# Exponentials ahead of the copies of transposed probabilities, and the softmax's multiply ahead of their low parts, in a kernel of window attention and two feed-forward blocks

## The chip, the core and the metric

The kernel runs on one core of a Trainium2 chip. The metric is the device time of one execution in microseconds; the kernel before takes 861.66 us, the median of three runs (861.57 to 862.0).

## What is computed

Attention with a window of 64 positions over 4 sequences of 576 tokens and 8 heads of 64, then two feed-forward parts on the 2304 tokens. All is in 32-bit floats.

```python
scores = scale * np.matmul(q, k.transpose(0, 1, 3, 2))
mask = (rel >= 0) & (rel < window)
scores = np.where(mask, scores, -1000000000.0)
scores = scores - np.max(scores, axis=-1, keepdims=True)
attn = np.exp(scores)
attn = attn / (np.sum(attn, axis=-1, keepdims=True) + 1e-09)
x = np.matmul(attn, v)
...
a = x @ w1
b = x @ w2
h = a * b @ w3
x = h @ w_out
...
h = x @ w_in
g = h * (1.0 / (1.0 + np.exp(-h)))
out = g @ w_out2
```

## The kernel before

**Precision.** Most matrix products are made in three passes of a faster 32-bit format: an operand is split into a high part (a rounded copy, made on ScalarE) and a low part (operand minus high part, made on VectorE or GpSimd), and high x high, high x low and low x high are added up in PSUM. In the trace the high parts are CAST instructions, the low parts TENSOR_TENSOR instructions with a subtraction.

**Attention** goes in 72 groups: a group is 128 queries of one pair of heads against 192 keys, and 12 groups are one block of 384 tokens. Groups 0 to 16 are plain: their products are ordinary 32-bit ones with no low parts. The work of group g is cut into two halves, written by half(h):

- The even half of g issues scores(g) on TensorE (L272, L276, or L268 in plain groups) and their masked maxima on VectorE (L282); values(g - 2), the product of transposed probabilities pt and values (L349, L350, or L342 to L344); the three transposes of g - 1 into the PSUM tile t (L315); split_t(g - 1), which copies t to pt on ScalarE (L325, L327) and takes the low parts on VectorE (L328, two of L330), or in plain groups one copy to pw (L321); and exps(g), the two exponentials on ScalarE (L293).
- The odd half of g issues normalise(g) on VectorE: a reduction (L301), a reciprocal (L303) and the multiply of the probabilities by it (L305); then the pending total of values(g - 2): two copies on ScalarE (L357, L358), two sums on VectorE (L359, L360) and one add on GpSimd into xr (L361). Then prep_qk (a cast on ScalarE, L247; low parts on GpSimd, L251, and VectorE, L254), prep_v (vhl: L79 on ScalarE, L82 on GpSimd) and the loads on SyncE's queue. In the last group of a block the total stands in the even half instead, behind the exponentials, because the next block needs xr.

**The rest.** phase_w, the front stage, rebuilds the weights from 64-bit words on ScalarE, VectorE and GpSimd and multiplies w3 with w_out (L492), with 28 halves in between. Then come six blocks of the first feed-forward part, phase_a: 16 units of 12 matmuls (L520) whose product is a = (x w1)(x w2), made on VectorE (L528) and split into p or q by ScalarE (L79) and GpSimd (L82); then 8 units of 12 matmuls (L540) with the combined weights, while the next block's xr is split into xa and xb. Ahead of each unit, unit(n) issues one half of attention, so a block carries 24 halves, 12 groups. The attention ends within the fifth block (block 4); the second feed-forward part (L640, L659) follows and fills the rest.

**Order.** The program is scheduled by hand: every engine runs its instructions in the order in which they are written, and waits at the first whose inputs or buffers are not ready. pt and the probabilities sm have two buffers each, t has one.

Of the kernel before, what the change touches and what calls it, by code (L numbers as in the profile page):

```python
# [14 lines left out]
ALU = mybir.AluOpType  # L15
# [27 lines left out]
def tile_window_attention_ffn(ctx, tc, qkv, vp, mask, ident, w1, w2, w3t, w_out, w_in, w_out2, out):  # L43
# [7 lines left out]
    nc = tc.nc  # L51
# [7 lines left out]
    def f32(ap):  # L59
        return ap.bitcast(F32)  # L60
# [99 lines left out]
    def fill(n=1):  # L160

        for _ in range(min(n, len(parts))):
            parts.pop(0)()
# [24 lines left out]
    NG = NU * NPAIR  # L188
# [14 lines left out]
    HEADS = (0, slice(0, 64)), (1, slice(64, 128))  # L203
# [4 lines left out]
    def plain(g):  # L208


        return g < PLAIN
# [20 lines left out]
    def load_v(g):  # L232
        if g < NG and ("v", g) not in loaded:
            loaded.add(("v", g))
            if plain(g):
                nc.sync.dma_start(out=v_p[g % 3], in_=vp[g])
                return
            v_raw[g] = att.tile([128, 3, 64], F32, name=f"v{g}", tag="v", bufs=3)
            u, c = place(g)
            nc.sync.dma_start(out=v_raw[g].rearrange("p t d -> p (t d)"), in_=qkv[u, c, :, 768:960])  # L240

    def prep_qk(g):
        if g >= NG or plain(g):
            return
        t = qk_raw.pop(g)
        hi = att.tile([128, 768], F32R, name=f"qkhi{g}", tag="qkhi", bufs=2)
        nc.scalar.copy(out=hi, in_=t)  # L247
        q, k = slice(128, 384), slice(384, 768)
        for h, hs in HEADS:
            n = slice(384 + h * 192, 576 + h * 192)  # L250
            nc.gpsimd.tensor_tensor(  # L251
                out=k_lo[g % 2][hs, h * 192 : h * 192 + 192], in0=t[hs, n], in1=f32(hi[hs, n]), op=ALU.subtract
            )
        nc.vector.tensor_tensor(out=hi[64:128, q], in0=t[64:128, q], in1=f32(hi[64:128, q]), op=ALU.subtract)  # L254
        qk_st[g] = hi

    def prep_v(g):
        if plain(g):
            return
        vhl = att.tile([128, 3, 2, 64], F32R, name=f"vhl{g}", tag="vhl", bufs=2)  # L260
        split(vhl[:, :, 0], vhl[:, :, 1], v_raw.pop(g), "act", "pool")
        v_st[g] = vhl

    def scores(g):
        s_ps = psa.tile([128, 2, 192], F32, name=f"s{g}", tag="s")
        t = qk_raw.pop(g) if plain(g) else qk_st.pop(g)
        if plain(g):
            nc.tensor.matmul(s_ps, lhsT=t[:, 0:128], rhs=k_p[g % 2], start=True, stop=True)  # L268
        else:
            for h in range(2):  # L270

                nc.tensor.matmul(  # L272
                    s_ps[:, h], lhsT=t[:, 128 + h * 128 : 256 + h * 128],
                    rhs=t[:, 384 + h * 192 : 576 + h * 192], start=(h == 0), stop=False,
                )
            nc.tensor.matmul(s_ps, lhsT=t[:, 0:128], rhs=k_lo[g % 2], start=False, stop=True)  # L276
        nm = att.tile([128, 2], F32, name=f"nm{g}", tag="nm", bufs=2)
        rs = att.tile([128, 2], F32, name=f"rs{g}", tag="rs", bufs=2)
        fill(2)
        for h in range(2):  # L280

            nc.vector.tensor_tensor_reduce(  # L282
                out=sm[g % 2][:, h, :], in0=s_ps[:, h, :], in1=mask_sb[:, mask_kind(place(g)[0]), 64 - 64 * h : 256 - 64 * h],
                op0=ALU.add, op1=ALU.min, scale=-(D ** -0.5), scalar=3.0e38, accum_out=nm[:, h : h + 1],
            )
        fill()
        s_st[g] = (nm, rs)

    def exps(g):
        nm, rs = s_st[g]  # L290
        for h in range(2):
            x = sm[g % 2][:, h, :]
            nc.scalar.activation(  # L293
                out=x, in_=x, func=AF.Exp, scale=-1.0, bias=nm[:, h : h + 1], accum_out=sums_of[g % 2][:, h, 0:1]
            )

    def normalise(g):
        _, rs = s_st.pop(g)
        x = sm[g % 2]
        fill()  # L300
        nc.vector.tensor_reduce(out=rs, in_=sums_of[g % 2], axis=mybir.AxisListType.X, op=ALU.add)  # L301
        fill()
        nc.vector.reciprocal(out=rs, in_=rs)  # L303
        fill()
        nc.vector.tensor_tensor(out=x, in0=x, in1=rs.unsqueeze(2).to_broadcast([128, 2, 192]), op=ALU.mult)  # L305

    def transposes(g):

        x = sm[g % 2]
        t_ps = psa.tile([128, 384], F32, name=f"t{g}", tag="t")
        x = x.rearrange("p h n -> p (h n)")
        for i, at in enumerate((0, 256, 128)):
            nc.tensor.transpose(t_ps[:, i * 128 : i * 128 + 128], x[:, at : at + 128], id_sb)  # L315
        return t_ps

    def split_t(g, t_ps):
        if plain(g):
            p_st[g] = p_w[g % 2]  # L320
            nc.scalar.copy(out=p_st[g], in_=t_ps[:, 0:320])  # L321
            return
        b, a = pt[g % 2, 1], pt[g % 2, 0]
        own, before = t_ps[:, 0:256].rearrange("p (h n) -> p h n", h=2), t_ps[:, 256:320]
        nc.scalar.copy(out=b[:, :, 0, :], in_=own)  # L325
        for h, hs in HEADS:
            nc.scalar.copy(out=a[hs, h, 0], in_=before[hs])  # L327
        nc.vector.tensor_tensor(out=b[:, :, 1, :], in0=own, in1=f32(b[:, :, 0, :]), op=ALU.subtract)  # L328
        for h, hs in HEADS:
            nc.vector.tensor_tensor(out=a[hs, h, 1], in0=before[hs], in1=f32(a[hs, h, 0]), op=ALU.subtract)  # L330

    def values(g):
        u, c = place(g)
        r = u % 3 * 128

        tag = "z" if done["step"] == len(line) and g % 2 else "o"
        o_ps = psa.tile([128, 2, 2, 128], F32, name=f"o{g}", tag=tag)
        if plain(g):


            v, p, o = v_p[g % 3], p_st.pop(g), o_ps[:, 0, 0]
            nc.tensor.matmul(o, lhsT=v[:, 0:128], rhs=p[:, 0:128], start=True, stop=False)  # L342
            nc.tensor.matmul(o, lhsT=v[:, 64:192], rhs=p[:, 128:256], start=False, stop=False)
            nc.tensor.matmul(o[:, 0:64], lhsT=v[:, 192:320], rhs=p[:, 256:320], start=False, stop=True)  # L344
            return lambda: nc.scalar.copy(out=xr[:, c, r : r + 128], in_=o)
        vhl = v_st.pop(g)
        b, a = pt[g % 2, 1], pt[g % 2, 0]
        for h in range(2):
            nc.tensor.matmul(o_ps[:, h], lhsT=vhl[:, h], rhs=b[:, h], start=(h == 0), stop=False)  # L349
        nc.tensor.matmul(o_ps[:, :, :, 0:64], lhsT=vhl[:, 2], rhs=a, start=False, stop=True)  # L350
        o_ps = o_ps.rearrange("p h t n -> p h (t n)")

        def total():
            t = att.tile([128, 256], F32, name=f"ot{g}", tag="ot", bufs=1)
            if g == NG - 1:
                att.tile([128, 24], F32, name="odd_end", tag="odd_end", bufs=1)
            nc.scalar.copy(out=t[0:64], in_=o_ps[64:128, 0, :])  # L357
            nc.scalar.copy(out=t[64:128], in_=o_ps[0:64, 1, :])  # L358
            nc.vector.tensor_tensor(out=t[0:64], in0=o_ps[0:64, 0, :], in1=t[0:64], op=ALU.add)  # L359
            nc.vector.tensor_tensor(out=t[64:128], in0=o_ps[64:128, 1, :], in1=t[64:128], op=ALU.add)  # L360
            nc.gpsimd.tensor_tensor(out=xr[:, c, r : r + 128], in0=t[:, 0:128], in1=t[:, 128:256], op=ALU.add)  # L361

        return total

    def half(h):

        g, odd = divmod(h, 2)
        if not odd:  # L370
            if g < NG:
                scores(g)
            if 2 <= g <= NG + 1:
                sums.append(values(g - 2))
                if plain(g - 2):
                    sums.pop()()
            if 1 <= g <= NG:
                split_t(g - 1, transposes(g - 1))
            if g < NG:
                exps(g)  # L380
            if sums and (g - 2) % (3 * NPAIR) == 3 * NPAIR - 1:
                sums.pop()()
        else:
            if g < NG:
                normalise(g)
            if sums:
                sums.pop()()
            prep_qk(g + 2)
            if g < NG:
                prep_v(g)  # L390

            for x in range(g + 2, g + 5):
                if plain(x) and x > g + 2:
                    break
                load_qk(x)
            for x in range(g + 1, g + 4):
                if g < (x - 1 if plain(x - 3) else x - 3):
                    break
                load_v(x)

    halves, sums = [0], []

    def halves_to(n):
        while halves[0] < min(n, LAST_HALF):
# [364 lines left out]
```

## Time and profile before

| | |
|---|---|
| median of three runs | 861.66 us |
| the profiled execution, its own time | 861.8 us |
| its span | 860.0 us |
| TensorE matmul, busy | 842.0 us, 98% |
| TensorE weight load, busy | 736.7 us, 86% |
| VectorE, busy | 435.8 us, 51% |
| ScalarE, busy | 497.7 us, 58% |
| GpSimd, busy | 445.0 us, 52% |
| granted TensorE clock | 1.0 of full speed throughout |

Busy time is the share of the span in which an engine worked on instructions; register and waiting instructions don't count. The ends of matmuls are modelled, so that a TensorE that reads as busy may still wait for a fraction of a microsecond; the starts of its weight loads show that better. In the rows, PE is TensorE's matmul, PEld its weight load, DVE is VectorE, ACT ScalarE, POOL GpSimd.

### The profile page before, as it was taken

The numbers are of one execution on the slowest core, as the hardware profiler recorded it, in microseconds if no ns is written. First come the engines' busy times: TensorE is split into PE (matmuls) and PEld (weight loads), VectorE is DVE, ScalarE is ACT, GpSimd is POOL, SyncE is SP. The second block draws the span as 40 slices with busy tenths as digits, with TensorE's granted clock in tenths as the row PEclk, the third lists the DMA queues.
The fourth block names the chain that finished last, engine by engine and source line by source line (L and its number), as shares of the span: only waits on it lengthen the run. The fifth ranks groups of instructions, "written<-read, shape, count | busy, mean of one in ns | idle before, by whom it ended". The sixth has DMA issues, their size and how long they took to land.

```text
span 860.0 us, 13396 instructions
## 1 busy us (share of the span) xinstructions
PE 842.0 (98%) x4362; PEld 736.7 (86%) x4362; DVE 435.8 (51%) x1160; ACT 497.7 (58%) x1243; POOL 445.0 (52%) x494
## 2 busy tenths in 40 slices
PE   5899999999999999999999999999999999999998
PEld 2455799999999999999999888888888888888896
DVE  5979877677777777676465985111111111111111
ACT  5889778788788788787666874222222222222222
POOL 4668666566666666665595886223322232223222
PEclk9999999999999999999999999999999999999999
DMA  8988333333333334330687200200020002000100
GB/s 289 349 272 276 104 105 102 121 93 108 114 93 111 111 94 125 111 94 30 233 326 263 116 1 0 98 1 1 0 98 1 1 0 74 1 1 0 50 1 26
DMA packets 43205, 85.84 MB, mean 100 GB/s; under 512 B 4864, under 2 KB 22528, under 8 KB 43136
## 3 DMA queue, kind: packets, MB, share of 16 engines
q1 hardware_dynamic: 37088, 75.55, 26.7%
q10 hardware_dynamic: 6048, 9.44, 3.0%
q8 instruction: 35, 0.57, 0.3%
q14 instruction: 34, 0.28, 0.1%
HBM read 75.53 MB, written 9.44 MB: 99 GB/s over the span
## 4 chain that ended last, share of the span: by engine, by line
PE 86%; DVE 1%; ACT 1%; issue 1%; POOLq 0%; POOL 0%; ACTq 0%; DVEq 0%
PE h L640 23%; PE o L659 23%; PE ab L520 22%; PE x L540 12%; PE t L315 2%; PE o L349 1%; PE s L272 1%; PE s L276 1%; PE o L350 1%; ACT sm L293 0%; DVE a L528 0%; DVE sm L305 0%; DVE cv_b L128 0%; POOLq L765 0%; DVE hl L144 0%
## 5 line engine op out<-in xcount | busy, mean ns | idle before, releaser
L82 POOL TENSOR_TENSOR g<-sg,g 128x512 fp32r<-128x512 f32 (+1 forms) x80 | 94.7, 1184 | 244.8 <-ACT g L79 217.7
L640 PE MATMUL h<-x2t,hl 128*128 128x512 f32 (+1 forms) x960 | 210.1, 368 | 0.0
L659 PE MATMUL o<-hl,g 128*128 128x512 f32 x864 | 209.7, 390 | 0.1
L640 PEld LDWEIGHTS h<-x2t,hl 128*128 128x128 f32 x960 | 169.3, 188 | 31.2
L646 DVE TENSOR_TENSOR sg<-h,sg 128x512 f32<-128x512 f32 (+1 forms) x80 | 51.1, 638 | 283.7 <-ACT sg L645 283.6
L659 PEld LDWEIGHTS o<-hl,g 128*128 128x128 f32 x864 | 161.1, 188 | 33.5 <-POOL g L82 0.5
L645 ACT ACTIVATE sg<-h 128x512 f32<-128x512 f32 (+1 forms) x80 | 44.4, 555 | 190.0 <-PE h L640 189.7
L520 PE MATMUL ab<-xa,hl 128*128 128x384 f32 x576 | 119.0, 341 | 0.0
L520 PE MATMUL ab<-xb,hl 128*128 128x384 f32 x576 | 115.3, 334 | 0.0
L520 PEld LDWEIGHTS ab<-xb,hl 128*128 128x128 f32 x576 | 101.2, 188 | 0.0
L520 PEld LDWEIGHTS ab<-xa,hl 128*128 128x128 f32 x576 | 99.2, 188 | 0.0
L132 POOL TENSOR_TENSOR cv_b<-cv_b,cv_r 128x512 int32<-128x512 int32 x48 | 73.5, 1531 | 19.1 <-DVE cv_b L128 8.1
L79 ACT CAST g<-sg 128x512 fp32r<-128x512 f32 (+1 forms) x80 | 46.3, 579 | 63.5 <-DVE sg L646 63.5
L361 POOL TENSOR_TENSOR xr<-ot 128x128 f32<-128x128 f32 x55 | 31.6, 575 | 98.3 <-DVE ot L360 67.2
L251 POOL TENSOR_TENSOR klo<-qk,qkhi 64x192 fp32r<-64x192 f32 x110 | 67.4, 613 | 7.6 <-ACT qkhi L247 2.7
L540 PE MATMUL x<-p,wp 128*128 128x384 f32 x360 | 68.0, 339 | 0.0
L293 ACT ACTIVATE sm<-sm,nm 128x192 f32<-128x192 f32 x144 | 64.5, 450 | 3.9 <-DVE nm L282 2.5
L540 PEld LDWEIGHTS x<-p,wp 128*128 128x128 f32 x360 | 61.7, 188 | 0.1
L125 DVE TENSOR_SCALAR cv_z<-cv_b 128x512 int32<-128x512 int32 x72 | 49.4, 686 | 15.7 <-ACT cv_b L114 14.7
L114 ACT ACTIVATE cv_b<-words 128x512 f32<-128x512 f32 x72 | 48.3, 671 | 12.2 <-DMA words<-in_w_out 4.6
L128 DVE SCALAR_TENSOR_TENSOR cv_b<-words,cv_z 128x512 int32<-128x512 int32 x72 | 49.5, 687 | 3.3
L115 ACT ACTIVATE cv_r<-words 128x512 int32<-128x512 uint32 x72 | 47.8, 664 | 0.0
(81 smaller groups left out, 1236.5 us busy)
## 6 DMA issues: line engine op xcount, KB each, us to landing
qk<-in_qkv SPq DMA_DIRECT2D x55, 384.0 KB, 3.1
words<-in_w_out SPq DMA_DIRECT2D x24, 512.0 KB, 8.0
words<-in_w3t SPq DMA_DIRECT2D x16, 512.0 KB, 6.4
words<-in_w SPq DMA_DIRECT2D x16, 512.0 KB, 6.4
words<-in_w_in SPq DMA_DIRECT2D x16, 512.0 KB, 6.7
v<-in_qkv SPq DMA_DIRECT2D x55, 96.0 KB, 2.7
x2d<-x2s ACTq DMA_DIRECT2D x24, 192.0 KB, 1.9
out_x<-osb ACTq DMA_DIRECT2D x18, 256.0 KB, 2.1
```

The costliest lines, as they stand in the source:

```text
L82: (nc.vector if eng_lo == "dve" else nc.gpsimd).tensor_tensor(out=lo, in0=src, in1=f32(hi), op=ALU.subtract)
L114: nc.scalar.activation(out=f32(self.b), in_=f32(self.high), func=AF.Copy, scale=2.0**-112)
L125: nc.vector.tensor_scalar(out=self.z, in0=b, scalar1=3, scalar2=None, op0=ALU.logical_shift_left)
L128: nc.vector.scalar_tensor_tensor(out=b, in0=self.high, scalar=-0x80000000, in1=self.z, op0=ALU.bitwise_and, op1=ALU.bitwise_or)
L132: nc.gpsimd.tensor_tensor(out=x, in0=b, in1=self.r, op=ALU.add)
L251: nc.gpsimd.tensor_tensor(out=k_lo[g % 2][hs, h * 192 : h * 192 + 192], in0=t[hs, n], in1=f32(hi[hs, n]), op=ALU.subtract)
L293: nc.scalar.activation(out=x, in_=x, func=AF.Exp, scale=-1.0, bias=nm[:, h : h + 1], accum_out=sums_of[g % 2][:, h, 0:1])
L520: nc.tensor.matmul(acc, lhsT=w[:, l, fs], rhs=x[k // 2][:, k % 2, r, :], start=(k == 0 and n == 0), stop=(k == 3 and n == 2),)
L540: nc.tensor.matmul(acc, lhsT=wp[f][:, l, o * 128 : (o + 1) * 128], rhs=p[f][:, r, :], start=(f == 0 and n == 0), stop=(f == 7 and n == 2),)
L640: nc.tensor.matmul(acc, lhsT=weights["in", f // 4, k][:, l, fs], rhs=x[:, k, r, :], start=(k == 0 and i == 0), stop=(k == 3 and i == 2),)
L646: nc.vector.tensor_tensor(out=sg, in0=acc, in1=sg, op=ALU.mult)
L659: nc.tensor.matmul(oacc[t], lhsT=g[:, l, t * 128 : (t + 1) * 128], rhs=weights["out", f][:, r, :], start=(f == 0 and i == 0), stop=(f == 1 ...
```

## The change

half() now calls exps(g) ahead of split_t(g - 1), so that on ScalarE the exponentials stand in front of the copies out of t. split_t issues the copies only and returns its three low parts as a function, low(), which is kept in the list lows; the odd half calls it behind normalise(g). So on VectorE the reduction, reciprocal and multiply of g stand in front of the low parts of g - 1. Plain groups have no low parts, and only ScalarE's order changes in them.

```diff
@@ split_t @@
             p_st[g] = p_w[g % 2]
             nc.scalar.copy(out=p_st[g], in_=t_ps[:, 0:320])
-            return
+            return lambda: None
...
-        nc.vector.tensor_tensor(out=b[:, :, 1, :], in0=own, in1=f32(b[:, :, 0, :]), op=ALU.subtract)
-        for h, hs in HEADS:
-            nc.vector.tensor_tensor(out=a[hs, h, 1], in0=before[hs], in1=f32(a[hs, h, 0]), op=ALU.subtract)
+
+        def low():
+            nc.vector.tensor_tensor(out=b[:, :, 1, :], in0=own, in1=f32(b[:, :, 0, :]), op=ALU.subtract)
+            for h, hs in HEADS:
+                nc.vector.tensor_tensor(out=a[hs, h, 1], in0=before[hs], in1=f32(a[hs, h, 0]), op=ALU.subtract)
+
+        return low
@@ half @@
-            if 1 <= g <= NG:
-                split_t(g - 1, transposes(g - 1))
+            t_ps = transposes(g - 1) if 1 <= g <= NG else None
             if g < NG:
                 exps(g)
+            if t_ps is not None:
+                lows.append(split_t(g - 1, t_ps))
             if sums and (g - 2) % (3 * NPAIR) == 3 * NPAIR - 1:
                 sums.pop()()
         else:
             if g < NG:
                 normalise(g)
+            if lows:
+                lows.pop()()
             if sums:
                 sums.pop()()
```

The line numbers in the orders of the changed kernel are its own: its L330 and L332 are the low parts (L328 and L330 before), L361 to L364 the total (L357 to L360 before), L533 and L535 are L526 and L528 before.

VectorE in one group of block 2, from the low parts of one group (those of t_2200) to the maxima of the next. First before, then now; a name's number only tells buffers apart.

```order
L328 TENSOR_TENSOR pt_976<-t_2200,pt_976 128x2x128
L330 TENSOR_TENSOR pt_974<-t_2200,pt_974 64x64 x2
L301 TENSOR_REDUCE rs_2193<-es_81 128x2
L303 RECIPROCAL rs_2193<-rs_2193 128x2
L305 TENSOR_TENSOR sm_72<-sm_72,rs_2193 128x384
L359 TENSOR_TENSOR ot_2230<-o_2196,ot_2230 64x256
L360 TENSOR_TENSOR ot_2230<-o_2196,ot_2230 64x256
L254 TENSOR_TENSOR qkhi_2236<-qk_2092,qkhi_2236 64x256
```

```order
L301 TENSOR_REDUCE rs_2193<-es_81 128x2
L303 RECIPROCAL rs_2193<-rs_2193 128x2
L305 TENSOR_TENSOR sm_72<-sm_72,rs_2193 128x384
L330 TENSOR_TENSOR pt_976<-t_2200,pt_976 128x2x128
L332 TENSOR_TENSOR pt_974<-t_2200,pt_974 64x64 x2
L363 TENSOR_TENSOR ot_2230<-o_2196,ot_2230 64x256
L364 TENSOR_TENSOR ot_2230<-o_2196,ot_2230 64x256
L254 TENSOR_TENSOR qkhi_2236<-qk_2092,qkhi_2236 64x256
```

The three low parts moved from ahead of the softmax's three steps to behind them, directly ahead of the two sums.

ScalarE in the same group, from the high part of p to the first copy of the total: before, then now.

```order
L79 CAST p_1882<-a_3_2149 128x384
L325 CAST pt_976<-t_2200 128x2x128
L327 CAST pt_974<-t_2200 64x64 x2
L293 ACTIVATE sm_72,es_81<-sm_72,nm_2192 128x192 x2
L526 COPY a_4_2225<-ab_8_2212 128x384
L357 COPY ot_2230<-o_2196 64x256
```

```order
L79 CAST p_1882<-a_3_2146 128x384
L293 ACTIVATE sm_72,es_81<-sm_72,nm_2192 128x192 x2
L325 CAST pt_976<-t_2200 128x2x128
L327 CAST pt_974<-t_2200 64x64 x2
L533 COPY a_4_2222<-ab_8_2209 128x384
L361 COPY ot_2230<-o_2196 64x256
```

The two exponentials moved ahead of the three copies; what stands behind the five is the same. TensorE's, GpSimd's and SyncE's orders are as before.

## Rows read from the trace of the kernel before

**Rows 1.** Busy time by stretch: the stretch, its length, PE, PEld, DVE, ACT, POOL.

```profile
200.00:300.00 100.00, 100.00 (x627) 99.39 (x626) 73.19 (x258) 81.89 (x248) 63.26 (x96) 1.00 0.36 110
```

**Rows 2.** Timeline of one group in block 2: start us, us, engine, line, operation.

```profile
239.67 0.43 DVE L360 TENSOR_TENSOR ot<-o,ot 64x256 f32<-64x256 f32 x1
...
240.18 0.60 POOL L361 TENSOR_TENSOR xr<-ot 128x128 f32<-128x128 f32 x1 [1.85 <-DVE ot L360]
...
241.49 0.37 ACT L325 CAST pt<-t 128x256 fp32r<-128x256 f32 x1
...
242.08 0.60 POOL L82 TENSOR_TENSOR vhl<-v,vhl 128x192 fp32r<-128x192 f32 x1
242.22 0.46 ACT L293 ACTIVATE sm<-sm,nm 128x192 f32<-128x192 f32 x1
242.23 0.42 DVE L328 TENSOR_TENSOR pt<-t,pt 128x256 fp32r<-128x256 f32 x1 [0.64 <-ACT pt L327]
...
242.57 0.45 DVE L330 TENSOR_TENSOR pt<-t,pt 64x64 fp32r<-64x64 f32 x2
...
242.64 1.01 POOL L82 TENSOR_TENSOR p<-a,p 128x384 fp32r<-128x384 f32 x1
...
243.63 0.56 DVE L305 TENSOR_TENSOR sm<-sm,rs 128x384 f32<-128x384 f32 x1
...
244.54 0.37 PEld L349 LDWEIGHTS o<-pt,vhl 128*128 128x128 f32 x2
244.58 0.42 DVE L359 TENSOR_TENSOR ot<-o,ot 64x256 f32<-64x256 f32 x1 [0.39 <-ACT ot L358]
...
244.84 0.19 PEld L350 LDWEIGHTS o<-pt,vhl 128*128 128x128 f32 x1
...
245.01 0.43 DVE L360 TENSOR_TENSOR ot<-o,ot 64x256 f32<-64x256 f32 x1
```

**Rows 3.** Timeline, second half of block 1: a multiply that meets a GpSimd operation.

```profile
215.79 1.02 POOL L82 TENSOR_TENSOR xa<-xr,xa 128x384 fp32r<-128x384 f32 x1
...
216.27 0.95 DVE L305 TENSOR_TENSOR sm<-sm,rs 128x384 f32<-128x384 f32 x1
217.25 0.42 DVE L359 TENSOR_TENSOR ot<-o,ot 64x256 f32<-64x256 f32 x1
```

**Rows 4.** Timeline: the values' last weight load, two groups earlier than in rows 2.

```profile
234.33 0.19 PEld L350 LDWEIGHTS o<-pt,vhl 128*128 128x128 f32 x1
```

**Rows 5.** Timeline, end of the first half of block 2.

```profile
269.32 1.01 POOL L82 TENSOR_TENSOR q<-a,q 128x384 fp32r<-128x384 f32 x1
...
270.38 0.30 PEld L540 LDWEIGHTS x<-q,wp 128*128 128x128 f32 x2 [0.30 <-POOL q L82]
...
271.37 0.19 PEld L350 LDWEIGHTS o<-pt,vhl 128*128 128x128 f32 x1
```

**Rows 6.** Timeline, the seam between blocks 1 and 2.

```profile
223.06 0.56 DVE L305 TENSOR_TENSOR sm<-sm,rs 128x384 f32<-128x384 f32 x1
...
223.82 0.19 PEld L350 LDWEIGHTS o<-pt,vhl 128*128 128x128 f32 x1
```

**Rows 7.** Timeline, end of the front stage: copy and exponentials of a plain group.

```profile
110.31 0.43 ACT L321 COPY pw<-t 128x320 f32<-128x320 f32 x1
...
110.63 0.47 ACT L293 ACTIVATE sm<-sm,nm 128x192 f32<-128x192 f32 x1
```

**Rows 8.** Waits: who waited for whom: us in total, times, longest.

```profile
ACT sm L293 <- DVE nm L282: 2.5, 3, 1.5
...
PE t L315 <- ACT cv_r L115: 1.8, 2, 1.0
PE t L315 <- ACT cv_b L114: 1.6, 1, 1.6
PE t L315 <- DVE sm L305: 1.0, 2, 0.7
```

More of the change, by code (lines that the diff above doesn't have):

```diff
@@ L399, in half @@
                 load_v(x)
-    halves, sums = [0], []
+    halves, sums, lows = [0], [], []
     def halves_to(n):
```

## Prediction, written before the changed kernel was run

> **What bounds the kernel now.** I read the busy share by stretch first. Between 200 and 300 us TensorE is busy all the time and its weight loads fill 99.39 of 100 us, while VectorE shows 73.19, ScalarE 81.89 and GpSimd 63.26 [rows 1]. At first sight nothing that happens on the other three can matter from the first feed-forward block on, and only the front stage, where the weights are rebuilt, has waits on TensorE. The timeline of one group of attention in block 2 says how far that holds [rows 2]. Read it as a ring: VectorE's second sum of head outputs (L360) at 239.67 lets GpSimd start its add (L361, which had idled 1.85 us for it); GpSimd then works down its queue to the low part of p, 242.64 to 243.65; ScalarE copies the transposed probabilities from 241.49, runs the exponentials from 242.22; VectorE takes the low parts at 242.23, the softmax's multiply at 243.63, the sums from 244.58, and at 245.01 it is at L360 again. One round is 245.01 - 239.67 = 5.34 us. TensorE needs (244.84 - 234.33) / 2 = 5.255 us a group [rows 2, 4]. So the ring is already slower than TensorE by 0.08 us a group, and lives on slack: the values' last weight load (L350, 244.84) needs low parts that ended at 242.57 + 0.45 = 243.02, 1.8 us of slack, and the multiply, which the transposes right behind that load need, ended at 243.63 + 0.56 = 244.19, 0.65 us ahead of it. At the end of the block's first half the slack is gone: a weight load of the second half waits 0.30 us for GpSimd's low part of q [rows 5]. That the ring is not at its own limit by busy time, and yet TensorE waits for it, is what I build on.
>
> **The change part by part.** Nothing is added or removed: no instruction, no DMA. TensorE's, GpSimd's and SyncE's queues keep their order. Two things move.
>
> *ScalarE, all groups.* The two exponentials go ahead of the copies. In the group shown the copies take 242.22 - 241.49 = 0.73 us, so the exponentials start 0.73 us earlier and everything behind the pair (a, the head outputs' copies) stands where it stood. The maxima that the exponentials need are there: VectorE sat idle for 0.64 us ahead of 242.23, so it was through with both by 241.59, and the first head's come first. This costs nothing there.
>
> *VectorE, groups 17 and up.* The softmax's three steps go ahead of the three low parts. Exponentials to multiply took 243.63 - 242.22 = 1.41 us, so the multiply is now ready at 241.49 + 1.41 = 242.90 us. But GpSimd's low part of p runs from 242.64 to 243.65. What a multiply does that comes up while such a GpSimd operation runs, a row of block 1 shows [rows 3]: begun at 216.27 under an operation that ended at 215.79 + 1.02 = 216.81, it took 0.95 us instead of 0.56 and ended at 217.22, 0.41 us after GpSimd's. It waited for the whole operation. So the multiply, moved forward by 0.73 us, ends at 243.65 + 0.41 = 244.06, only 0.13 us earlier than the 244.19 of before. The low parts did not wait under GpSimd's vhl (0.42 us at 242.23, beside 242.08 to 242.68), so they add 242.57 + 0.45 - 242.23 = 0.79 us, and start 0.03 us behind the multiply as L359 does at 217.25: they end at 244.88, not at 243.02. This is the price: 1.8 us of slack go, while the multiply gains 0.13.
>
> Two waits follow. First, the last weight load of the values stands at 244.84 and its low parts now end at 244.88. Second, the sums (L359, 244.58, so far released by ScalarE) come at 244.80 to 244.88; the earlier end is for an overlap of 0.08 us such as L330's with L328. That is 0.22 to 0.30 us later, and the sums are the ring's next step. The ring's round becomes 5.56 to 5.64 us, with GpSimd and VectorE wholly in line: L360, GpSimd's four steps to p, the multiply, the low parts, L359, L360. The multiply cannot slip ahead of p, because p starts 242.64 - 239.67 = 2.97 us behind L360 and the multiply is ready 3.23 us behind it, round by round.
>
> *Per block.* The ring meets p or q eight times in the first half of a block (first about 231.97, two rounds ahead of the 242.64 shown; last 269.32; 37.35 / 5.34 = 7 rounds between). The first time the low parts end about 234.21, just ahead of the load at 234.33. The last time, with no growth, they end at 269.32 + 1.01 + 0.41 + 0.03 + 0.79 = 271.56; with seven rounds' growth of 0.22 to 0.30 us at 273.10 to 273.66. The load that needs them stood at 271.37 [rows 5], with the 0.30 us of waiting for q already in it. So TensorE is 1.73 to 2.29 us later per block. I take 1.75, by the lower end, because the nearest row for one low part behind another shows the overlap. In the second half of a block p's splitting is gone, the multiply meets shorter waits, and the ring catches up as before.
>
> At the seam between blocks the order differs: the sums stand ahead of the softmax there, and the multiply ran 223.06 to 223.62 with the values' load at 223.82 [rows 6]. The low parts behind it now end at 223.65 + 0.79 = 224.44, so TensorE waits 0.4 to 0.6 us (less if the exponentials' earlier start pulls the multiply along). The ring is not held up by that, so I don't add it: it only uses up slack that the growing ring takes anyway.
>
> Four blocks (1 to 4) have this: 4 x 1.75 = **+7.0 us**. Block 0 has split groups only in its later part; at 0.3 us a group over some four it could cost up to 1.2; TensorE has just been stopped there and the slack is fresh, so I take nothing.
>
> *The front stage.* Groups 0 to 16 have no low parts; only ScalarE's order changes. The plain copy stands 110.63 - 110.31 = 0.32 us ahead of the exponentials [rows 7]; that is the most a group can gain. It counts only where TensorE waits for transposes: 1.8 + 1.6 + 1.0 = 4.4 us in all [rows 8], which includes one before any copy exists. In three groups ScalarE waited for VectorE ahead of the exponentials, 2.5 us in all [rows 8]; there the copy filled idle time and now delays what follows by about its 0.43 us: at most 3 x 0.43 = 1.3 us lost. Bounds: 4.4 gained, 1.3 lost. I take 0.3 gained, the last wait for transposes of that stage, whose copy and exponentials are shown [rows 7].
>
> Sum against the profiled execution: 861.8 + 7.0 - 0.3 = 868.5 us. That execution is 0.14 us above the median of 861.66, so the forecast is **868.4 us**.
>
> **The rivals.**
> A (forecast): the ring slows; 868.4, and 861.66 + 4 x 2.29 = 870.8 by its upper bound with nothing from the front. Chance 0.62.
>
> B: the ring does not slow, because the multiply starts ahead of p or the low parts fit beside ScalarE's copies, and only the seams cost: 4 x 0.4 to 0.6 = 1.6 to 2.4, so about 863.3 to 864.1. For it: the margin between p's start and the multiply is only 0.26 us. Against: both hang on the same L360. Chance 0.22.
>
> C: nothing changes, 861.7: TensorE stays full, and 1.8 us of slack or some rest of it covers all. The Trainium skill, Perfetto Trace Analysis, section Identifying the Most-Contended Engine, would have it so: it takes occupancy as a fair measure for VectorE, ScalarE and GpSimd and looks for gains at the engine with the highest. Here that is TensorE. The trace does not bear it out in one place: TensorE waits for GpSimd's q [rows 5] though GpSimd is busy 63 us in 100. Chance 0.10.
>
> D, on the other side: the front stage is what counts. Each group's transposes wait for a multiply that waits for the exponentials; started 0.32 us earlier in most of the 17 groups they could take back most of 4.4 us, less the first wait of about 1 us, so about 858.4. It decides if VectorE's low parts in the blocks still end ahead of the values' loads. Against: long transfers and conversions, not the copies, stand in most of those waits. Chance 0.06.
>
> **How the numbers follow.** The likeliest case gives 868.4. The range, 863.4 to 870.8, runs from B's floor to A's upper bound; left out are C, D and a few per cent of A beyond. A measurement of this kernel can tell about 0.2%, 1.7 us. Slower by more: A and nearly all of B above 863.4, 0.83. Within: C and a rest of B, 0.12. Faster: 0.05, of D.
>
> **What would show it.** Right: in the first half of the blocks, VectorE's multiply at 1.1 us or more, ending 0.41 us behind GpSimd's p; TensorE waits at L349 and L350 for the low parts, some 0.3 us a group from the second or third group of a block on; L360 to L360 at 5.56 to 5.64; the wait for q gone; waits of 0.4 to 0.6 us at four seams. Wrong: a multiply of 0.56 us there, TensorE without waits from 115 to 410 us, or a difference that arises before 115 us.

## The result, and the profile after

The changed kernel takes 867.47 us (median of six runs, 866.58 to 868.68), the kernel before, timed beside it, 861.64 us. The ratio is 1.007 with a 95% interval of 1.0059 to 1.008: 5.8 us slower, where 6.7 more than the 861.66 us of before was forecast. The profiled execution has a span of 866.9 us against 860.0.

The timeline of the changed kernel, for the group that answers to [rows 2] (its L330 and L332 are the low parts, L363 and L364 the sums, L353 and L354 the values' weight loads):

```profile
242.24 0.43 DVE L364 TENSOR_TENSOR ot<-o,ot 64x256 f32<-64x256 f32 x1
...
242.75 0.58 POOL L365 TENSOR_TENSOR xr<-ot 128x128 f32<-128x128 f32 x1 [2.09 <-DVE ot L364]
...
243.63 0.52 ACT L79 CAST p<-a 128x384 fp32r<-128x384 f32 x1 [1.18 <-DVE a L535]
...
244.05 0.45 ACT L293 ACTIVATE sm<-sm,nm 128x192 f32<-128x192 f32 x1
...
244.93 0.35 ACT L325 CAST pt<-t 128x256 fp32r<-128x256 f32 x1
245.06 0.16 DVE L301 TENSOR_REDUCE rs<-es 128x2 f32<-128x4 f32 x1 [0.92 <-ACT sm L293]
...
245.20 1.01 POOL L82 TENSOR_TENSOR p<-a,p 128x384 fp32r<-128x384 f32 x1
...
245.45 1.17 DVE L305 TENSOR_TENSOR sm<-sm,rs 128x384 f32<-128x384 f32 x1
245.65 0.48 ACT L533 COPY a<-ab 128x384 f32<-128x384 f32 x1
...
246.52 0.36 ACT L362 COPY ot<-o 64x256 f32<-64x256 f32 x1
246.54 0.41 DVE L330 TENSOR_TENSOR pt<-t,pt 128x256 fp32r<-128x256 f32 x1
...
246.87 0.45 DVE L332 TENSOR_TENSOR pt<-t,pt 64x64 fp32r<-64x64 f32 x2
...
247.20 0.37 PEld L353 LDWEIGHTS o<-pt,vhl 128*128 128x128 f32 x2
247.35 0.42 DVE L363 TENSOR_TENSOR ot<-o,ot 64x256 f32<-64x256 f32 x1
...
247.49 0.19 PEld L354 LDWEIGHTS o<-pt,vhl 128*128 128x128 f32 x1
...
247.78 0.43 DVE L364 TENSOR_TENSOR ot<-o,ot 64x256 f32<-64x256 f32 x1
```

The multiply comes up at 245.45, 0.25 us into GpSimd's low part of p, and ends at 246.62, 0.41 us after it: 1.17 us where it took 0.56. The wait stands inside the multiply's own time; the profile shows a longer instruction, and no idle time ahead of it. In blocks 1 to 4 all eight multiplies that meet p or q in the first half of a block take 1.14 to 1.18 us. The low parts, now behind the multiply, end at 247.32; the sums follow at 247.35, with ScalarE's copy for them (L362, which ended at 246.88) no longer what they wait for. The last weight load of the values starts at 247.49, 0.17 us behind the end of its low parts, where it had 1.8 us of slack. It does not yet wait: it stands 0.29 us behind L353, as L350 stood 0.30 behind L349. A round from L364 to L364 is 5.54 us, against 5.34.

At the seam between blocks 1 and 2, where [rows 6] stood:

```profile
225.01 0.56 DVE L305 TENSOR_TENSOR sm<-sm,rs 128x384 f32<-128x384 f32 x1
225.60 0.42 DVE L330 TENSOR_TENSOR pt<-t,pt 128x256 fp32r<-128x256 f32 x1
225.94 0.45 DVE L332 TENSOR_TENSOR pt<-t,pt 64x64 fp32r<-64x64 f32 x2
226.14 0.30 PEld L353 LDWEIGHTS o<-pt,vhl 128*128 128x128 f32 x2 [0.38 <-issue]
...
226.50 0.19 PEld L354 LDWEIGHTS o<-pt,vhl 128*128 128x128 f32 x1
```

The weight loads of the values wait for the low parts, 0.38 us of it in the row of L353. The profile names no releaser ("issue"); the times do: L353 starts 0.12 us behind the end of L330, L354 0.11 us behind the end of L332. The same distances stand at the end of the first half of block 2:

```profile
268.72 0.41 DVE L330 TENSOR_TENSOR pt<-t,pt 128x256 fp32r<-128x256 f32 x1
...
269.06 0.45 DVE L332 TENSOR_TENSOR pt<-t,pt 64x64 fp32r<-64x64 f32 x2
...
269.25 0.30 PEld L353 LDWEIGHTS o<-pt,vhl 128*128 128x128 f32 x2 [0.16 <-issue]
...
269.62 0.19 PEld L354 LDWEIGHTS o<-pt,vhl 128*128 128x128 f32 x1
```

From the sixth to the tenth group of blocks 1 to 4, and at their seams, L354 starts 0.11 to 0.12 us behind its low parts; in the kernel before the same distance was never under 1.49 us.

Where in the program the time goes is read from the starts of one weight load per group (L350 before, L354 after), one trace against the other, 55 groups. These are differences of rows, in us: 0.61 throughout block 0, 1.13 behind the first seam, 1.10 through four groups, then 1.33, 1.63, 1.90, 2.18; 2.68 behind the second seam, 3.77 at the end of block 2's first half, 5.33 at block 3's, 6.89 at the end of the attention and of the run. So each of blocks 1 to 4 adds 1.57 us: 0.51 at the seam and 1.06 in the later part of its first half. Four times 1.57 is 6.28 us, against 5.8 between the medians (5.1 to 6.9 by the interval). The 0.61 ahead of block 0 was there at the first multiply already (15.84 against 15.11), before any instruction that the change moves: it belongs to the two executions, not to the change.

The wait for q, 0.30 us once a block before [rows 5], is left once, at 0.2 us; TensorE itself now comes later. The waits of TensorE's weight loads between 100 and 420 us, after:

```profile
PEld o L353 <- issue: 2.3, 9, 0.4
PEld t L315 <- PE o L348: 0.4, 1, 0.4
PEld x L547 <- POOL q L82: 0.2, 1, 0.2
```

The first line has 2.3 us, where the starts show 6.28: most of the loss does not appear as idle time of the weight loads.

### The profile page after: what moved, and what is told of

The parts are those of the page before. It is cut to its first block, busy times and chain, and to the rows that moved or that the text cites. A ratio compares the mean times of both kernels' runs of the same rounds, so it can differ in the third digit from the quotient of the medians.

```text
span 866.9 us, 13334 instructions
## 1 busy us (share of the span) xinstructions
PE 850.4 (98%) x4362; PEld 739.3 (85%) x4362; DVE 452.8 (52%) x1160; ACT 492.9 (57%) x1243; POOL 446.3 (51%) x494
## 4 chain that ended last, share of the span: by engine, by line
PE 70%; POOL 10%; issue 5%; DVE 1%; ACT 1%; POOLq 0%; ACTq 0%; DVEq 0%
PE h L647 23%; PE o L666 22%; PE ab L527 16%; PE x L547 5%; POOL klo L251 4%; POOL vhl L82 2%; POOL xr L365 2%; PE t L315 1%; POOL xa L82 1%; PE o L353 1%; POOL q L82 1%; POOL p L82 1%; PE s L272 1%; PE s L276 1%; PE o L354 1%
## 5 line engine op out<-in xcount | busy, mean ns | idle before, releaser
L305 DVE TENSOR_TENSOR sm<-sm,rs 128x384 f32<-128x384 f32 x72 | 66.8, 928 | 2.5
```

## The experiments

The ring theory of the prediction says: VectorE's sums (L359, L360) start GpSimd's round; whatever stands ahead of them on VectorE lengthens the round once it ends behind ScalarE's copies, and the multiply costs 1.17 us instead of 0.56 where it meets GpSimd. Each run below puts a rival to it.

**Each half of the change alone.** ScalarE's half, with the low parts at their old place:

```diff
             if g < NG:
                 exps(g)
             if t_ps is not None:
-                lows.append(split_t(g - 1, t_ps))
+                split_t(g - 1, t_ps)()
```

> ScalarE's half of the change alone: exponentials ahead of the copies, VectorE's low parts ahead of the softmax as before. Ring theory (low parts and multiply stand in line ahead of the sums, and the sums start GpSimd's next round): the copies end at 243.2 in the group shown, the low parts at 244.0, then reduction, reciprocal and the multiply, 244.4 to 245.0, so the sums come 0.4 us later and a round takes about 5.75 us; the multiply no longer meets p and takes 0.56. TensorE about 3 us later per block: 872 to 875. Rival, the two moves' harm lies in VectorE's order alone: as before, 861 to 862.

Measured: 874.97 us, ratio 1.0152 (1.0136 to 1.0167). Its timeline, one group:

```profile
242.11 1.01 POOL L82 TENSOR_TENSOR p<-a,p 128x384 fp32r<-128x384 f32 x1
242.58 0.42 DVE L330 TENSOR_TENSOR pt<-t,pt 128x256 fp32r<-128x256 f32 x1 [1.51 <-ACT pt L327]
242.92 0.45 DVE L332 TENSOR_TENSOR pt<-t,pt 64x64 fp32r<-64x64 f32 x2
...
243.79 0.56 DVE L305 TENSOR_TENSOR sm<-sm,rs 128x384 f32<-128x384 f32 x1
...
244.38 0.42 DVE L363 TENSOR_TENSOR ot<-o,ot 64x256 f32<-64x256 f32 x1
244.47 0.31 PEld L315 LDWEIGHTS t<-id_sb,sm 128*128 128x128 f32 x3 [0.39 <-PE o L354]
```

VectorE idles 1.51 us for copies that now stand behind the exponentials, and the transposes' weight load (L315) starts 0.39 us late, 0.12 us behind the multiply that ended at 244.35. Between 100 and 420 us there are 34 such waits:

```profile
PEld t L315 <- PE o L354: 12.0, 34, 0.4
```

The profile puts them down to the matmul before; by the rows it is the multiply. The low parts, in one stretch with p (242.58 to 243.37 beside 242.11 to 243.12), did not wait for GpSimd: 0.42 us and 0.45 as ever.

VectorE's half:

```diff
+            if t_ps is not None:
+                lows.append(split_t(g - 1, t_ps))
             if g < NG:
                 exps(g)
-            if t_ps is not None:
-                lows.append(split_t(g - 1, t_ps))
```

> VectorE's half alone: copies ahead of the exponentials as before, low parts behind the multiply. Ring theory: the multiply stays at 243.63 (exponentials unmoved) with 0.56 us, since p is just over; the low parts end at 245.0, the sums start 0.35 to 0.42 us later, a round takes 5.7 us; 871 to 875. Rival, the waiting for GpSimd's p is the whole of the loss: no such wait here, so within 1 us of before.

Measured: 874.53 us, ratio 1.0147 (1.0132 to 1.0162).

```profile
242.87 1.01 POOL L82 TENSOR_TENSOR p<-a,p 128x384 fp32r<-128x384 f32 x1
...
243.86 0.56 DVE L305 TENSOR_TENSOR sm<-sm,rs 128x384 f32<-128x384 f32 x1
244.33 0.42 DVE L330 TENSOR_TENSOR pt<-t,pt 128x256 fp32r<-128x256 f32 x1
244.67 0.45 DVE L332 TENSOR_TENSOR pt<-t,pt 64x64 fp32r<-64x64 f32 x2
...
245.15 0.42 DVE L363 TENSOR_TENSOR ot<-o,ot 64x256 f32<-64x256 f32 x1
```

The multiply does not meet p here and still the kernel is the slower one: the exponentials hold the multiply, and the low parts stand behind both. TensorE waits at the values' loads instead of the transposes':

```profile
PEld o L353 <- issue: 8.6, 29, 0.6
```

In the first half of the blocks a round is 5.65 us in the first run and 5.66 in the second, by the sums' rows. Each half alone costs some 13 us, both together 5.8: the rivals that lay the blame on one of the moves fall.

**GpSimd's low part of p out of the multiply's way.** In the changed kernel, it is issued behind the next group's add into xr (all but the last of a block):

```diff
-                split(p[f][:, 0], p[f][:, 1], a_sb[:, 1], "act", "pool")
+                if f == 7 or blk == NBLK - 1:
+                    split(p[f][:, 0], p[f][:, 1], a_sb[:, 1], "act", "pool")
+                else:
+                    nc.scalar.copy(out=p[f][:, 0], in_=a_sb[:, 1])
+                    later.append((p[f], a_sb))
...
             if sums:
                 sums.pop()()
+            while later:
+                t, s = later.pop()
+                nc.gpsimd.tensor_tensor(out=t[:, 1], in0=s[:, 1], in1=f32(t[:, 0]), op=ALU.subtract)
             prep_qk(g + 2)
```

> The changed kernel with GpSimd's low part of p (all but the last of a block) put behind the next group's add into xr, so that it no longer runs when the multiply comes up. Ring theory: the multiply takes under 0.9 us, the low parts end ahead of ScalarE's copies, a round is back at 5.33 to 5.36; waits at the seams stay: 862.5 to 864.5. Rival, the low parts' place behind the softmax costs by itself, wherever p stands: a round stays at 5.5, about 867.5.

Measured: 864.21 us, ratio 1.003 (1.002 to 1.0039). That is 2.5 us above the 861.74 of before beside it, where the change cost 5.8. Its timeline:

```profile
249.43 1.27 POOL L251 TENSOR_TENSOR klo<-qk,qkhi 64x192 fp32r<-64x192 f32 x2
...
250.62 0.56 DVE L305 TENSOR_TENSOR sm<-sm,rs 128x384 f32<-128x384 f32 x1
...
250.78 0.86 POOL L82 TENSOR_TENSOR vhl<-v,vhl 128x192 fp32r<-128x192 f32 x1
...
251.09 0.42 DVE L330 TENSOR_TENSOR pt<-t,pt 128x256 fp32r<-128x256 f32 x1
```

The multiply takes 0.56 us and now it is GpSimd's vhl that comes up 0.16 us into it and takes 0.86 instead of 0.60. Within blocks 1 to 4 TensorE keeps its distance to before to within 0.03 us; only the seams are left, 0.51 us each, and about 0.1 us at the end of a block's first half, where TensorE waits for q (0.44 us in block 0). The low parts' place behind the softmax costs nothing by itself inside a block when p is away: the rival falls, and the meeting with p is what costs there. What I had not forecast: a round is 5.24 to 5.25 us, TensorE's own pace, and not 5.33.

**The seams.** In the changed kernel, the old order on VectorE in a block's last group alone:

```diff
             if sums and (g - 2) % (3 * NPAIR) == 3 * NPAIR - 1:
+                if lows:
+                    lows.pop()()
                 sums.pop()()
```

> The changed kernel with the old order of VectorE in the last group of a block only (low parts, total, softmax). Ring theory: the 0.5 us at each of four seams disappear, but the ring goes on growing from the same place, so TensorE waits that much longer within the block: 867.0 to 867.6. Rival, the waits add up: four times 0.5 less, 865.4.

Measured: 866.47 us, ratio 1.0054 (1.0039 to 1.0069). Neither: the jump at the seams is gone and a block adds 1.30 us instead of 1.57, by the same weight loads as above (0.25 at block 1's end, 1.54 at block 2's, 2.86, 4.17). Of the 0.51 us at a seam 0.24 were taken up again within the block, as the ring theory has it, and 0.27 were a loss of their own. The sums' rows show why. At the seam between blocks 1 and 2, first the changed kernel, then this one:

```profile
224.16 0.43 DVE L364 TENSOR_TENSOR ot<-o,ot 64x256 f32<-64x256 f32 x1
...
231.11 0.43 DVE L364 TENSOR_TENSOR ot<-o,ot 64x256 f32<-64x256 f32 x1
```

```profile
222.25 0.43 DVE L364 TENSOR_TENSOR ot<-o,ot 64x256 f32<-64x256 f32 x1
...
228.94 0.43 DVE L364 TENSOR_TENSOR ot<-o,ot 64x256 f32<-64x256 f32 x1
```

From a seam's L364 to the next is 6.95 us in the changed kernel and 6.69 in this one (6.79 in the kernel before), so the ring was held up too.

**The front stage.** In the kernel before, the new order of ScalarE in the plain groups alone (exps ahead of split_t where g - 1 is plain, as before elsewhere; split_t returns its low parts as in the change):

```diff
-            if 1 <= g <= NG:
-                split_t(g - 1, transposes(g - 1))
+            t_ps = transposes(g - 1) if 1 <= g <= NG else None
+            if t_ps is not None and not plain(g - 1):
+                split_t(g - 1, t_ps)()
+                t_ps = None
             if g < NG:
                 exps(g)
+            if t_ps is not None:
+                lows.append(split_t(g - 1, t_ps))
...
```

> The kernel before with the new order on ScalarE in the plain groups alone; the split groups as before. By the prediction's term the front stage gains 0.3: 861.4, no more than the spread. Rival, the front stage as such loses 0.6, as the profile of the changed kernel shows ahead of the first block: 862.3. Rival D of the prediction, a gain of up to 3.4: 858.4.

Measured: 861.47 us, ratio 0.9999 (0.9987 to 1.001). And the reverse, the changed kernel with the old order in its plain groups:

```diff
+            if t_ps is not None and plain(g - 1):
+                lows.append(split_t(g - 1, t_ps))
+                t_ps = None
             if g < NG:
                 exps(g)
```

> The changed kernel with the old order in the plain groups. If all the loss lies in blocks 1 to 4 (1.57 us each): 861.7 + 6.3 = 868.0 with no front effect, so the same as the changed kernel within 0.5. Rival, the front costs 0.6: 866.9.

Measured: 868.32 us, ratio 1.0068 (1.0056 to 1.0081), as the changed kernel. Neither run shows a part of the front stage in the result. Both intervals reach about 1 us either way, so rival D's gain of 3.3 us and a loss as large as the whole are ruled out; a gain of 0.3 us is not. The 0.61 us of the profiled execution is spread: the four profiled executions of the first experiments came into block 0 between 1.05 us earlier and 1.70 us later than before's.

**A version that takes the gain.** The changed order in the split groups, p's low part moved for the first six of a block (f < 6), the old order at the seams and in the plain groups; and beside it the kernel before with p moved in the same way, as control. The lines for p, in both:

```diff
-                split(p[f][:, 0], p[f][:, 1], a_sb[:, 1], "act", "pool")
+                if f >= 6 or blk == NBLK - 1:
+                    split(p[f][:, 0], p[f][:, 1], a_sb[:, 1], "act", "pool")
+                else:
+                    nc.scalar.copy(out=p[f][:, 0], in_=a_sb[:, 1])
+                    later.append((p[f], a_sb))
```

> The changed order in the split groups, with GpSimd's low part of p behind the next group's add for the first six of a block, the old order at the seams and in the plain groups. Ring theory: a round is 5.25 as with p later, TensorE never waits for low parts, the 0.5 us at the seams is gone, and with the ring no slower than TensorE the 0.3 us wait for q at the end of a block's first half goes too: 4 x 0.27 below before, 860.6. Rival, q now comes late by the moved p as in the run with p later: 861.7 to 862.2.

Measured: 860.26 us, ratio 0.9979 (0.9971 to 0.9988): 0.2% faster, 1.7 us below the 861.94 of before beside it. In its profiled execution the weight loads gain 0.25 to 0.28 us on before at the end of the first half of blocks 1 to 4, where TensorE had waited for q [rows 5], 1.04 us in all; another 0.54 us was there ahead of block 0, within the spread of executions. A round is 5.20 us at the start of a block, up to 5.26 later in its first half, and 5.55 to 5.57 once, where the multiply meets the q that is not moved.

```profile
243.07 0.42 DVE L363 TENSOR_TENSOR ot<-o,ot 64x256 f32<-64x256 f32 x1 [0.28 <-ACT ot L362]
...
244.91 0.51 ACT L547 CAST p<-a 128x384 fp32r<-128x384 f32 x1 [0.83 <-DVE a L543]
```

The ring is here again one of ScalarE and VectorE (ScalarE waits 0.83 us for a, the sums 0.28 us for ScalarE's copy), as it was before, but with the exponentials first. The stretch from p's cast to the next copy on ScalarE shows what the order is worth. In the kernel before:

```profile
241.07 0.51 ACT L79 CAST p<-a 128x384 fp32r<-128x384 f32 x1 [0.82 <-DVE a L528]
...
243.23 0.48 ACT L526 COPY a<-ab 128x384 f32<-128x384 f32 x1
```

It took 2.16 us there, 2.02 in the changed kernel (243.63 to 245.65) and 2.03 in this run (239.70 to 241.73). In the old order the exponentials started 0.02 us behind the end of the copies (242.22 behind 242.20) and the next copy 0.02 us behind the exponentials (243.23 behind 243.21); in the new one the copies start 0.10 us ahead of the end of the exponentials (244.93 against 245.03), and the next copy 0.02 us behind the copies (245.65 behind 245.63). The difference is about the 0.14 us by which the round became shorter; no run changed this alone with the rest of the ring as it was.

> The kernel before with only GpSimd's low part of p moved, as control for e7. Ring theory: the ring of before is ScalarE's and VectorE's, 5.33 a round, and p's place is not in it; the wait for q stays: 861.4 to 862.0. Rival, moving p alone brings whatever e7 brings: 860.6.

Measured: 863.74 us, ratio 1.0019 (1.001 to 1.0028), 2 us above what I expected. One row a block says why:

```profile
265.47 0.60 POOL L82 TENSOR_TENSOR vhl<-v,vhl 128x192 fp32r<-128x192 f32 x1
266.02 1.02 POOL L82 TENSOR_TENSOR q<-a,q 128x384 fp32r<-128x384 f32 x1
266.06 1.40 DVE L305 TENSOR_TENSOR sm<-sm,rs 128x384 f32<-128x384 f32 x1
...
267.57 0.31 PEld L315 LDWEIGHTS t<-id_sb,sm 128*128 128x128 f32 x3 [0.46 <-issue]
```

This low part, of q, is the first of a block that is not moved; it follows a moved one and runs late, just ahead of the multiply: the multiply ends 0.42 us behind it at 267.46, and the transposes' weight load waits 0.46 us. The other rounds of the first half are as before (5.33 to 5.34), so p was not in the ring of before. One such meeting per block costs 0.49 to 0.53 us in blocks 1 to 4 and 0.2 in block 0: the plainest measure of the cost that the forecast rested on. As a control the run is marred by that meeting, but no row of it gains on before. So, as far as these runs show, the gain of the version above needs both, the new order and p out of its way.

## Why the prediction was right

**The multiply's wait: right to 0.01 us.** Forecast 0.26 us into p, ending 0.41 us behind it, at 1.16 us; the rows show 0.25, 0.41 and 1.17. The Trainium skill, GPSIMD Engine Reference, section Key points, says that GpSimd shares its SBUF interfaces with VectorE and contends with instructions that have two SBUF inputs. The trace agrees: the multiply with both inputs in SBUF waits, the low parts with one input in PSUM do not (0.42 us beside p). The one that comes second waits for the whole of the other: whether the multiply came up 0.04, 0.25 or 0.48 us [rows 3] into the GpSimd operation, it ended 0.41 to 0.42 us behind it. Either may be the one that waits (0.86 for vhl behind a multiply).

**The ring: right, 0.02 us under the range.** 5.56 to 5.64 us a round were forecast, 5.54 measured. The low parts were to start 0.03 us behind the multiply, as the sums do [rows 3]; they started 0.08 ahead of its end (246.54 against 246.62). One thing was drawn wrong without harm: the prediction counts GpSimd's p among the steps of the ring of before. With p away that ring kept its 5.33 us; it was one of VectorE and ScalarE, and p came into it by the change.

**Per block: the mechanism right, the sum near by luck.** 1.75 us forecast, 1.57 measured; but the forecast was for the ring alone, and the run with the old order at the seams shows the ring alone at 1.30. Too much was taken for the ring, and nothing for the seams, where 0.27 was right. The ring's term had two sizes wrong. The growth was 0.20 us a round, not 0.22: 0.14 over seven rounds. And the low parts of the first meeting were to end 0.12 us ahead of their load (234.21 against 234.33); in that run it was 0.53:

```profile
233.58 0.45 DVE L332 TENSOR_TENSOR pt<-t,pt 64x64 fp32r<-64x64 f32 x2
...
234.56 0.19 PEld L354 LDWEIGHTS o<-pt,vhl 128*128 128x128 f32 x1
```

That is 0.41 us more slack to use up. The low parts' earlier start is 0.11 of it; the rest is a round that came 0.30 us earlier against TensorE, 0.1 of it won at the seam (6.69 against 6.79 before), 0.2 there already ahead of it (the L364 at 222.25 stood 0.04 us later than in the kernel before, TensorE 0.24). Against that, a load that waits starts 0.12 us behind its low parts: 1.73 - 0.14 - 0.41 + 0.12 = 1.30. The larger slack is also why the waits begin with the sixth group of a block, and not with the second or third.

**The seam: size right, consequence half wrong.** 0.4 to 0.6 forecast, 0.51 measured. "The ring is not held up by that" was the step that failed: the run with the old order there shows that it was, by 0.26, and that 0.27 of the 0.51 us are a loss of their own.

**Block 0 at nothing: right.** The distance to before stays at 0.61 us through all of it.

**The front stage: 0.3 us gained forecast, too small to measure** (ratio 0.9999, 0.9987 to 1.001). No run shows the gain, and none rules it out.

**The rivals.** B fell: p's place ahead of the multiply held in all eight rounds of a block's first half. C fell: TensorE waited for VectorE, which the changed kernel shows busy 75.84 of 100 us between 200 and 300. The Trainium skill, Perfetto Trace Analysis, section Identifying the Most-Contended Engine, has the engine with the highest occupancy optimised first. Here that is TensorE, whose order the change leaves alone, and the run was 5.8 us slower all the same. D fell with the front stage.

## What to carry to other kernels

Where one engine looks full, look at how far ahead of it the others finish at the end of the longest stretch, and not at their busy time: the kernel before lived on such a slack between its low parts and their load, which shrank by 0.08 us a group from 2.06 to 1.50 us over the first half of a block. Before an instruction is moved forward, look at what the engine that it contends with does at the new time: a move of 0.73 us gained 0.14 (the multiply ended 4.38 us behind the second sum, where it had been 4.52). And judge two orders that lean on each other together: each half alone cost over twice what both cost, and with GpSimd's part moved as well, and the old order at the seams, the pair was a gain.

## What the hardware showed that I had not expected

A GpSimd operation and a multiply of VectorE with both inputs in SBUF exclude each other both ways: 1.17 us instead of 0.56 for the multiply, 0.86 instead of 0.60 for GpSimd's, and 1.40 where an operation of 1.02 us started 0.04 us ahead of the multiply. And on ScalarE the mere order of exponentials and copies changed the same stretch of instructions from 2.16 to 2.02 us.
